# One core, attention beside a gated feed-forward: query loads issued one at a time, and new orders for the work of a unit

## The chip, the cores and the metric

The kernel runs on one NeuronCore of one Trainium2 chip. The metric is the device time of one execution in microseconds (us). Five engines run their own instruction streams in order and meet at semaphores: PE multiplies matrices (PEld is its weight load), DVE reduces, ACT applies exponentials and copies, POOL does elementwise work, and SP issues transfers between memory and the on-chip buffers.

## The reference

Both halves take the same x of 2048 tokens and 512 features, and everything is float32.

```
q = x @ wq   (32 heads of 16)      k = x @ wk, v = x @ wv  (one head of 16, shared)
p = softmax(q k^T / 4)             a = (p v) @ wo
b = ((x @ w_gate) * (x @ w_up)) @ w_down          (inner size 1792)
g = sigmoid(sum(x * gate_w))       out = g * a + (1 - g) * b
```

The scores are 32 x 2048 x 2048. Each needs its row's maximum first, then an exponential, then a product with v.

## The kernel before

**Units.** Attention is cut into 64 units. A unit `u` is eight heads (group `g`) of 128 query tokens (tile `t` of chunk `c`). Its queries stand in a buffer `Q[u]` with four slots of 128 columns in each of two halves of 64 partitions. There are `QB = 5` such buffers, so unit `u` reuses the buffer of unit `u - 5`.

**Three passes per unit.** `p1` multiplies queries with 512 keys (64 rows of the array, one half of the partitions) and DVE takes the row maximum (`mx`, L765 and L766). When 32 such tiles are done, `p1_end` folds them to one maximum per row, and SP writes it to memory in four pieces (`dm<-mt`, L786) and reads it back into two rows of each half of `Q[u]` (`Q<-dm`, L793). Thus `p2` computes score minus maximum in one product (L806), and ACT takes the exponential into `P` (L807). `pv` multiplies `P` with `V` into one bank `acc` (L819), four matrices side by side of 32 columns each, and ACT copies the result out as `osb` (L823).

**Fill.** Between these matmuls PE does the projections and the feed-forward as jobs (L965), each of which owns one of the eight PSUM banks until ACT has copied it (`gs`, L575, or `yt` and `y`, L399 and L396, which scale a result by its gate).

**The order.** PE's order is written out as strings of tokens. `a` and `b` are a `p1` matmul on the lower and the upper half of the partitions, `c` and `d` a `p2` matmul on these halves, `e` and `f` a fill matmul on them, and `p` is one step of `pv`, which the profile records as eight matmuls. Two matmuls on different halves run side by side; two on the same half follow each other. `ORDER` is one unit (144 tokens: 16 each of a, b, c and d, 36 each of e and f, 8 p). `ORDER_NINE` is a pair of units (288 tokens) and is used whenever a block of `down` jobs with nine products is ready (`nine_unit`), which happens for eight pairs. `ORDER_LAST` is the last pair. So 46 units follow `ORDER`, and 16 follow `ORDER_NINE`.

**The planner.** While the program is built, a planner keeps its own clock: each token advances it by fixed costs (`LANE` is the time between two matmuls of one half). Actions that aren't tokens, transfers among them, are put into a list by `later(ns, fn)` and are issued when that clock has passed. The clock is only an estimate: at run time SP issues its transfers in the order in which the planner recorded them, each when its semaphores allow.

**The query loads.** `place` calls `q_fetch(u)` when the buffer's old unit is through its `p2`. `q_fetch` issues two small transfers that clear the maximum rows (`Q<-dz`, L226) and six that bring the queries (`Q<-dq`, L233). It records in `qat` when the planner may count on them.

Of the kernel before, what the change touches and what calls it, by code (L numbers as in the profile page):

```python
# [14 lines left out]
F32 = mybir.dt.float32  # L15
# [7 lines left out]
DH = 16  # L23
# [9 lines left out]
PBUF = 13  # L33
WB = 4
QB = 5
LANE = 232.0
NEXT = 3.0
LOADW = 132.0
GAP = 50.0
# [9 lines left out]


ORDER = (
    "cdefedafcfebefedafeedafcfedebefadebefcfefefebededebefadfefcfadeefebedcfa"
    "fcfcfafefefafafcfefafcfedcfafafefedebcfebefebebebcbppppcdadcbppdababcppb"
)
ORDER_NINE = (
    "cbecffadeefdefafccfbeedbeefdafefcacfefebefebededaffebcefedafcffcfafefafe"
    "afdefedafecffeadcfefbedefadcpppdcdadcppcbcbadpppbcbcbefefcfefcfadedebede"
    "febcfebfefebedebedeebcfebedefafedefcfafcfafefedebafedefedfafecfaffcbefcf"
    "edadefafebefabapppadfcfebefcfedafefcbebefedefadefefebefcfabappbcbabapppb"
)  # L60
ORDER_LAST = (
    "cdebefebefefedededebbcfefefebefedaefefefadcfefafcfefafefedadefebefedefcf"
# [9 lines left out]
def mix_kernel(ctx: ExitStack, tc: tile.TileContext, x, wq, wk, wv, wo, wg, wu, wd, gw, out):  # L72
    nc = tc.nc
# [46 lines left out]
    clock = {"T": 0.0, "dve": 0.0, "act": 0.0, "pool": 0.0}  # L120
# [3 lines left out]
    def later(ns, fn):  # L124
        heapq.heappush(events, (clock["T"] + ns, next(serial), fn))
# [25 lines left out]
    def mm_all(p, prods, start=True, stop=True):  # L151
        for i, (l, r) in enumerate(prods):
            nc.tensor.matmul(p, l, r, start=start and i == 0, stop=stop and i == len(prods) - 1)  # L153
# [6 lines left out]
    def bank(i, name):  # L160
        return psum.tile([128, 512], F32, name=name, tag=f"bank{i}")

    def ms_bank(i):
        return bank(i, f"ms{i}")
# [51 lines left out]
    qat = {}  # L216

    Q = {u: work.tile([128, 4, 128], F32R, name="Q", tag="Q", bufs=QB) for u in range(QB)}
    dz = dram.tile([2, 512], F32, name="dz", bufs=1)

    def q_fetch(u):
        c, g, t = units[u]
        if u >= QB:
            Q[u] = Q[u - QB]
            for r in (48, 112):
                nc.sync.dma_start(Q[u][r:r + 2].rearrange("p s q -> p (s q)").bitcast(F32), dz)  # L226
        q = Q[u]
        for d, rows in zip(dq[c, g], ((0, 32), (16,))):
            for half in range(2):
                for r in rows:  # L230
                    b = half * 64 + r
                    src = d[half * 64:half * 64 + 64, t * 128:(t + 1) * 128]
                    nc.sync.dma_start(q[b:b + 16].bitcast(F32), src.rearrange("(s d) q -> d s q", d=DH))  # L233
        qat[u] = clock["T"] + 6000.0

    kvn = work.tile([128, 4, 32], F32, name="kvn", tag="oT", bufs=2)
    nc.scalar.dma_start(kvn[:, :, 0:16], wk_v)
# [209 lines left out]
    class State:  # L447
# [11 lines left out]
        def issue(self, l, wait):  # L459
# [3 lines left out]
            at = max(self.nl[l], self.last + NEXT, ldw + LOADW)  # L463
            self.nl[l] = at + LANE
            self.pd = max(ldw + 5.0, at - LANE)
            self.last = at
# [361 lines left out]
    p = bank(6, "warm")  # L828
# [3 lines left out]
    p = bank(6, "gwb")  # L832
# [8 lines left out]
    p = ms_bank(1)  # L841
# [3 lines left out]
    for u in range(2):  # L845
        q_fetch(u)
# [17 lines left out]
    p = ms_bank(0)  # L864
# [112 lines left out]
    def place(op):  # L977
        nonlocal fetched
        events_until(E.last if E.inpv else min(E.nl))
        if (fetched < NU and min(E.n2) >= NJ * (fetched - QB + 1) and fetched <= min(E.n1) // NJ + 2  # L980
                and (fetched != 3 or 0 in mat) and dqat.get(units[fetched][:2], 1e18) <= clock["T"]):
            later(1500, lambda n=fetched: q_fetch(n))
            fetched += 1
        if op == "p":
            at = E.npv
            E.pv()
            pv(at)
            return
        kind, l = divmod("abcdef".index(op), 2)
        if kind == 0:  # L990
            k = E.n1[l]
            if k < NS:
                wait_for(lambda: qat.get(order1[k][0], 1e18) <= clock["T"] + 200.0)
                b = E.s1(l)
                clock["dve"] = E.dve
                p1(k, l, b)
                E.dve = max(E.dve, clock["dve"])
                st["idle"] = min(E.n1) == NS
            elif fillable(l):
                fill(l)  # L1000
        elif kind == 1:
            k = E.n2[l]
            wait_for(lambda: mat.get(k // NJ, 1e18) <= clock["T"] + 200.0)
            p2(k, l, E.s2(l))
        elif not st["idle"] or fillable(l) or l == 1 and pos[1] < len(run):
            fill(l)
# [92 lines left out]
    while events or front or st["gen"] or st["next"]:  # L1099
        run_events()  # L1100
        if peek():
            j = take()
            items = j.prods()
            p = j.p
            if p is None:
                p = ms_bank(turn)
                turn = 1 - turn
            mm_all(p, items, j.start, j.evac is not None)
            clock["T"] += LANE * len(items)
            if j.evac:  # L1110
# [20 lines left out]
```

## Time and profile before

| | |
|---|---|
| median of 3 runs | 1583.41 us (1583.24 to 1583.56) |
| the profiled execution | 1583.97 us, its span 1582.2 us |
| PE, DVE, ACT, POOL busy | 1575.3, 1358.8, 1198.8, 734.5 us |
| L765, L806, L819, matmuls | 2048, 2048, 4096 |
| SP: `Q<-dq`, `Q<-dz`, `dm<-mt`, `Q<-dm` | 384, 118, 256 and 128 transfers |

A busy engine is not an engine at its best: the matmuls are pipelined, and a matmul that starts late shows as no idle time as long as the one before it is still running. Starts are therefore the better measure: the distance from one start to the next, and from the first `acc` of one unit to that of the next.

### The profile page before, as it was taken

What the parts mean: (1) busy time and instruction counts of PE and PEld (TensorE: products, weight loads), DVE (VectorE), ACT (ScalarE), POOL (GpSimd) and SP (SyncE); (2) the same over time, 40 slices, a digit from 0 to 9 for tenths busy, and PEclk for the clock granted to TensorE, in tenths of its full rate; (3) what the DMA queues carried; (4) which work ended last, traced back from release to release, by engine and by line L of the source; (5) the groups of instructions that cost most, each with busy time, mean ns of one, the idle gap of its engine ahead of it and who ended that gap; (6) DMA issues with size and microseconds to landing.
All of it is one profiled execution on the core that took longest, in us unless ns stands there. A gap on an engine that the chain in (4) does not pass through costs nothing.

```text
span 1582.2 us, 35723 instructions
## 1 busy us (share of the span) xinstructions
PE 1575.3 (100%) x13144; PEld 1026.6 (65%) x13144; DVE 1358.8 (86%) x2411; ACT 1198.8 (76%) x2384; POOL 734.5 (46%) x876
## 2 busy tenths in 40 slices
PE   9999999999999999999999999999999999999999
PEld 7775666665665666666665666676665666676665
DVE  6998989898888989898888889898888989898982
ACT  5786787877787787877787787877777786877776
POOL 8535636253633624454532625445443525545340
PEclk9999999999999999999999999999999999999999
DMA  6553322122232212121232212122132222212111
GB/s 197 188 177 119 94 63 74 43 69 60 68 104 80 75 49 74 43 87 55 61 104 72 75 56 74 50 69 66 55 117 65 69 61 75 61 57 59 36 32 42
DMA packets 185472, 121.71 MB, mean 77 GB/s; under 512 B 46435, under 2 KB 154851, under 8 KB 185298
## 3 DMA queue, kind: packets, MB, share of 16 engines
q1 hardware_dynamic: 184096, 119.10, 25.1%
q8 instruction: 104, 1.70, 0.4%
q14 instruction: 70, 0.57, 0.1%
q10 hardware_dynamic: 1202, 0.33, 0.1%
HBM read 83.18 MB, written 36.18 MB: 75 GB/s over the span
## 4 chain that ended last, share of the span: by engine, by line
PE 98%; DVE 1%; SPq 0%; issue 0%; DMA 0%; ACT 0%; POOL 0%; POOLq 0%
PE ms L965 33%; PE acc L819 29%; PE s L806 17%; PE s L765 17%; PE ms L153 1%; DVE mx L766 1%; PE ms L1055 1%; PE px L288 0%; SPq L233 0%; PE warm L830 0%; PE wo L153 0%; DMA Q<-dm 0%; PE pv L330 0%; SPq L786 0%; PE pick L730 0%
## 5 line engine op out<-in xcount | busy, mean ns | idle before, releaser
L766 DVE TENSOR_REDUCE mx<-s 128x1 f32<-128x512 f32 x2048 | 1285.1, 684 | 171.8 <-PE s L765 91.9
L807 ACT ACTIVATE P<-s 128x512 f32<-128x512 f32 x2048 | 1058.3, 648 | 258.8 <-PE s L806 217.3
L765 PE MATMUL s<-KK,Q 64*128 64x512 f32 x2048 | 702.5, 400 | 0.3
L806 PE MATMUL s<-Q,KK 64*128 64x512 f32 x2048 | 695.7, 404 | 1.5 <-DVE mx L766 0.8
L819 PE MATMUL acc<-P,V 128*32 128x512 f32 x4096 | 478.8, 597 | 0.0
L806 PEld LDWEIGHTS s<-Q,KK 64*128 64x128 f32 x2048 | 351.1, 184 | 133.0 <-ACT P L807 49.8
L765 PEld LDWEIGHTS s<-KK,Q 64*128 64x128 f32 x2048 | 350.5, 184 | 104.4 <-issue 52.0
L965 PE MATMUL ms<-xh,wl 64*128 64x512 f32 x896 | 314.6, 391 | 0.0
L965 PE MATMUL ms<-xh,wh 64*128 64x512 f32 x896 | 311.6, 392 | 0.0
L965 PE MATMUL ms<-xl,wh 64*128 64x512 f32 x896 | 300.4, 389 | 0.0
L819 PEld LDWEIGHTS acc<-P,V 128*32 128x32 f32 x4096 | 117.7, 109 | 254.2 <-issue 221.2
L586 POOL TENSOR_TENSOR hf<-gs 128x512 f32<-128x512 f32 x56 | 72.1, 1287 | 214.5 <-ACT gs L575 214.5
L965 PEld LDWEIGHTS ms<-xh,wh 64*128 64x128 f32 x896 | 159.2, 184 | 13.8 <-issue 0.5
L684 POOL TENSOR_TENSOR oT<-raw,rb 128x128 f32<-128x128 f32 x63 | 28.9, 459 | 288.2 <-DMA rb<-dr 279.2
L965 PE MATMUL ms<-wdh,hl 64*128 64x512 f32 x448 | 161.0, 391 | 0.0
L965 PEld LDWEIGHTS ms<-xh,wl 64*128 64x128 f32 x896 | 155.5, 184 | 7.6
L965 PE MATMUL ms<-wdh,hh 64*128 64x512 f32 x448 | 159.6, 390 | 0.0
L965 PEld LDWEIGHTS ms<-xl,wh 64*128 64x128 f32 x896 | 149.8, 184 | 8.8
L141 POOL TENSOR_TENSOR wl<-wn,wh 128x512 fp32r<-128x512 f32 x116 | 149.2, 1286 | 9.3
L400 POOL TENSOR_TENSOR y<-y,yt 128x512 f32<-128x512 f32 x58 | 74.7, 1288 | 169.3 <-ACT yt L399 160.7
L965 PE MATMUL ms<-wdl,hh 64*128 64x512 f32 x448 | 152.7, 390 | 0.0
L823 ACT COPY osb<-acc 128x512 f32<-128x512 f32 x64 | 37.6, 587 | 95.1 <-PE acc L819 95.1
(180 smaller groups left out, 1377.2 us busy)
## 6 DMA issues: line engine op xcount, KB each, us to landing
do<-osb SPq DMA_DIRECT2D x63, 256.0 KB
wn<-in_B_w_gate_dram SPq DMA_DIRECT2D x56, 256.0 KB
wn<-in_B_w_up_dram SPq DMA_DIRECT2D x56, 256.0 KB
wdn<-in_B_w_down_dram SPq DMA_DIRECT2D x56, 256.0 KB
Q<-dq SPq DMA_DIRECT2D x384, 32.0 KB
raw<-do SPq DMA_DIRECT2D x252, 32.0 KB
dq<-oh SPq DMA_DIRECT2D x16, 256.0 KB
dq<-ol SPq DMA_DIRECT2D x16, 256.0 KB
```

What stands on the lines that cost most here:

```text
L141: nc.gpsimd.tensor_tensor(lo, src, hi.bitcast(F32), op=OP.subtract)
L153: nc.tensor.matmul(p, l, r, start=start and i == 0, stop=stop and i == len(prods) - 1)
L400: nc.gpsimd.tensor_tensor(y[c, t], y[c, t], tmp, op=OP.add)
L586: nc.gpsimd.tensor_tensor(hf, gu[0], gu[1], op=OP.mult)
L684: nc.gpsimd.tensor_tensor(dst, raw[:, 0], rb, op=OP.mult)
L765: nc.tensor.matmul(p, q[r, slot], KK[r, kq * 512:(kq + 1) * 512], start=True, stop=True)
L766: nc.vector.tensor_reduce(mx[u][:, half * 4 + slot, kq:kq + 1], p, axis=AX.X, op=OP.max)
L806: nc.tensor.matmul(p, KK[r, j * 128:(j + 1) * 128], q[r].rearrange("p s q -> p (s q)"), start=True, stop=True)
L807: nc.scalar.activation(P[s][:, half], p, AF.Exp, scale=0.25)
L819: nc.tensor.matmul(acc[u][b:b + 32, :], V[:, j + i], src[:, half], start=(j == 0), stop=(j == NJ - 2))
L823: nc.scalar.copy(osb, acc.pop(u))
L965: nc.tensor.matmul(j.p, lhs[HALVES[l]], rhs[HALVES[l]], start=(l == 0 and i == 0), stop=(l == 1 and end))
```

## The change

`q_fetch` collects its two or no `dz` transfers and its six `dq` transfers in a list, issues the first, and puts each next one 1000 ns of the planner's clock behind the one before. (The first two units still issue all at once.) `qat` is 4000 ns behind the last one, not 6000 ns behind the burst. `LANE` goes from 232 to 229. `ORDER` and `ORDER_NINE` are replaced by other arrangements of the same tokens. No matmul, no reduction, no activation and no transfer is added or removed.

```
-LANE = 232.0
+LANE = 229.0
 ORDER = (
...
-    "fcfcfafefefafafcfefafcfedcfafafefedebcfebefebebebcbppppcdadcbppdababcppb"
+    "fcffafcfefafedefafebcfefcfafcfcfafebefcbefededebebcpppdcbcbappabcbcbpppb"
...
     def q_fetch(u):
         c, g, t = units[u]
+        parts = []
         if u >= QB:
             Q[u] = Q[u - QB]
             for r in (48, 112):
-                nc.sync.dma_start(Q[u][r:r + 2].rearrange("p s q -> p (s q)").bitcast(F32), dz)
+                parts.append((Q[u][r:r + 2].rearrange("p s q -> p (s q)"), dz))
...
-                    nc.sync.dma_start(q[b:b + 16].bitcast(F32), src.rearrange("(s d) q -> d s q", d=DH))
-        qat[u] = clock["T"] + 6000.0
+                    parts.append((q[b:b + 16], src.rearrange("(s d) q -> d s q", d=DH)))
+
+        def step(i):
+            nc.sync.dma_start(parts[i][0].bitcast(F32), parts[i][1])
+            if i + 1 < len(parts):
+                later(1000.0, lambda: step(i + 1))
+            else:
+                qat[u] = clock["T"] + 4000.0
+        if u >= 2:
+            step(0)
+        else:
+            for dst, src in parts:
+                nc.sync.dma_start(dst.bitcast(F32), src)
+            qat[u] = clock["T"] + 6000.0
```

The new file has 13 more lines ahead of the passes, so L786 reads L799 there, L819 reads L832, and so on.

**SP, the maxima of one early unit.** Here `dz` and `dq` are the query load of a later unit, and `dm` is the maximum on its way out (L786) and back (L793). Before:

```order
L226 DMA Q<-dz 2x512 x2
L233 DMA Q<-dq 16x4x128 x6
L786 DMA dm<-mt 8x2x32 x4
L179 DMA wn<-in_B_w_up_dram 128x4x128
L212 DMA dq<-oh 128x512
L212 DMA dq<-ol 128x512
L676 DMA dr<-rc 128x8
L793 DMA Q<-dm 2x512 x2
```

Now:

```order
L237 DMA Q<-dz 2x512
L179 DMA wn<-in_B_w_up_dram 128x4x128
L799 DMA dm<-mt 8x2x32 x4
L237 DMA Q<-dz 2x512
L237 DMA Q<-dq 16x4x128
L212 DMA dq<-oh 128x512
L212 DMA dq<-ol 128x512
L689 DMA dr<-rc 128x8
L237 DMA Q<-dq 16x4x128
L806 DMA Q<-dm 2x512 x2
```

Eight transfers of the query load stood ahead of the four writes of the maximum; now one does. Between the writes and the read back stand four other transfers before, and six now.

**PE, the end of a unit that follows ORDER.** `acc` rows count matmul instructions, four to a `p` token. Before:

```order
L819 MATMUL acc<-P,V 32x512 x16
L806 MATMUL s_2799<-Q,KK 128x512
L806 MATMUL s_2802<-Q,KK 128x512
L765 MATMUL s_2805<-KK,Q 128x512
L806 MATMUL s_2809<-Q,KK 128x512
L806 MATMUL s_2812<-Q,KK 128x512
L765 MATMUL s_2815<-KK,Q 128x512
L819 MATMUL acc<-P,V 32x512 x8
```

Now:

```order
L832 MATMUL acc<-P,V 32x512 x12
L819 MATMUL s_2791<-Q,KK 128x512
L819 MATMUL s_2795<-Q,KK 128x512
L778 MATMUL s_2798<-KK,Q 128x512
L819 MATMUL s_2801<-Q,KK 128x512
L778 MATMUL s_2804<-KK,Q 128x512
L778 MATMUL s_2807<-KK,Q 128x512
L832 MATMUL acc<-P,V 32x512 x8
```

Both go on with six matmuls and a third group, of 8 instructions before and of 12 now. A unit's eight steps of `pv` were grouped 4, 2, 2 and are grouped 3, 2, 3.

**PE, the end of the first unit of a pair that follows ORDER_NINE.** Before:

```order
L819 MATMUL acc<-P,V 32x512 x12
L806 MATMUL s_3551<-Q,KK 128x512
L806 MATMUL s_3554<-Q,KK 128x512
L806 MATMUL s_3558<-Q,KK 128x512
L765 MATMUL s_3561<-KK,Q 128x512
L806 MATMUL s_3565<-Q,KK 128x512
L806 MATMUL s_3568<-Q,KK 128x512
L819 MATMUL acc<-P,V 32x512 x8
L806 MATMUL s_3581<-Q,KK 128x512
```

Now:

```order
L832 MATMUL acc<-P,V 32x512 x12
L819 MATMUL s_3561<-Q,KK 128x512
L819 MATMUL s_3565<-Q,KK 128x512
L819 MATMUL s_3569<-Q,KK 128x512
L778 MATMUL s_3572<-KK,Q 128x512
L978 MATMUL ms_3432<-wdh,hh 128x512
L778 MATMUL s_3576<-KK,Q 128x512
L832 MATMUL acc<-P,V 32x512 x4
L819 MATMUL s_3585<-Q,KK 128x512
```

Before, the pair's groups of `pv` are 3, 2, 3 and 3, 2, 3 steps; now they are 3, 1, 2, 2 and 4, 2, 2, one group more. Two tokens of the same half stand side by side 27 times in the old pair and 47 times in the new one, 3 times and twice in the old and the new `ORDER`.

More of the change, by code (lines that the diff above doesn't have):

```diff
@@ L51 @@
 ORDER = (
-    "cdefedafcfebefedafeedafcfedebefadebefcfefefebededebefadfefcfadeefebedcfa"
-    "fcfcfafefefafafcfefafcfedcfafafefedebcfebefebebebcbppppcdadcbppdababcppb"
+    "cafedebedefedebedefadefcfafefadefedafcfafefebedefefadefcbefedebedafefeda"
+    "fcffafcfefafedefafebcfefcfafcfcfafebefcbefededebebcpppdcbcbappabcbcbpppb"
 )
 ORDER_NINE = (
[L56 to L59, printed above, removed]
+    "cfeadcfafefedefedafcfafedefedebefedafefbefedacfefcbeffcafefedafeffebdedf"
+    "eaebcfedefaefedafcfafefebedefcfebcfebcbpppdcdafapdcfabcppbcbcbeppcbfacff"
+    "eefbeedbefeddeaefedafedbefcfeedafcfebeffefebdfeebdecaeffcafdefafcbeedefe"
+    "dfacffafebfeceffadeafcffecfaffcfacfebefebedebebebcbppppdadcbappadcbabppb"
 )
```

## The prediction

> **What bounds the kernel now.** I read the page first, then the chain of waits, then single stretches.
>
> ```profile
> PE 1575.3 (100%) x13144; PEld 1026.6 (65%) x13144; DVE 1358.8 (86%) x2411; ACT 1198.8 (76%) x2384; POOL 734.5 (46%) x876
> PEclk9999999999999999999999999999999999999999
> PE 98%; DVE 1%; SPq 0%; issue 0%; DMA 0%; ACT 0%; POOL 0%; POOLq 0%
> ```
>
> PE carries the chain from end to end, at the full clock. The change adds no PE work, so it can only alter the distances between PE's starts. The chain in order of time shows each unit's first group of `acc`; two neighbours give a unit's length. Cut at such marks, the instructions on the tile `yt` (columns: stretch, its length, busy us and count on ACT, then on POOL, clock, DMA share, GB/s) show eight units that follow `ORDER`:
>
> ```profile
> 785.25 3.57 PE acc L819 x32
> 808.85 3.63 PE acc L819 x32
> ```
>
> ```profile
> 714.12:737.82 23.70, 1.48 (x2) 1.29 (x1) 1.00 0.21 60
> 737.82:761.63 23.81, 1.59 (x2) 3.87 (x3) 1.00 0.16 46
> 761.63:785.25 23.62, 0.00 (x0) 0.00 (x0) 1.00 0.26 71
> 785.25:808.85 23.60, 0.74 (x1) 0.00 (x0) 1.00 0.30 90
> 808.85:832.67 23.82, 2.37 (x3) 3.86 (x3) 1.00 0.37 113
> 832.67:856.51 23.84, 1.58 (x2) 3.87 (x3) 1.00 0.23 71
> 856.51:880.13 23.62, 0.00 (x0) 0.00 (x0) 1.00 0.24 69
> 880.13:903.76 23.63, 0.00 (x0) 0.00 (x0) 1.00 0.29 81
> ```
>
> Units without a `yt` take 23.62 us; of the four with two or three, one takes 23.70 and three 23.8, with the same work on PE. A `yt` is a longer copy on ACT, so ACT reaches PE although its mean share is 76%. The next rows (stretch, length, then busy us and count of PE, PEld, DVE, ACT, POOL) say where:
>
> ```profile
> 761.60:765.10 3.50, 3.50 (x34) 0.90 (x32) 3.42 (x8) 0.60 (x1) 2.17 (x3) 1.00 0.05 12
> 774.00:778.00 4.00, 4.00 (x38) 3.79 (x37) 4.00 (x7) 4.00 (x9) 1.18 (x1) 1.00 0.18 36
> 778.00:782.00 4.00, 4.00 (x39) 3.70 (x36) 3.99 (x7) 4.00 (x10) 3.78 (x5) 1.00 0.26 71
> ```
>
> In the first group of `pv`, four steps long, ACT has one instruction in 3.5 us: it starves. From 774 to 782 us ACT and DVE are both busy without a break. They catch up there, and a PSUM bank that either frees late delays the matmul that needs it. The mean share hides a starved stretch and a saturated one.
>
> **The price of a group, and the floor of a unit.** PE's starts in one of these units:
>
> ```profile
> 761.56 3.64 PE L819 MATMUL acc<-P,V 128*32 128x512 f32 x32
> ...
> 766.03 1.92 PE L819 MATMUL acc<-P,V 128*32 128x512 f32 x16
> ...
> 768.78 1.92 PE L819 MATMUL acc<-P,V 128*32 128x512 f32 x16
> 770.63 0.50 PE L765 MATMUL s<-KK,Q 64*128 64x512 f32 x1
> ...
> 770.97 0.62 PE L965 MATMUL ms<-xh,wh 64*128 64x512 f32 x2
> ...
> 773.05 0.39 PE L965 MATMUL ms<-xh,wh 64*128 64x512 f32 x1
> ...
> 774.19 0.39 PE L965 MATMUL ms<-xh,wh 64*128 64x512 f32 x1
> ...
> 784.86 0.39 PE L765 MATMUL s<-KK,Q 64*128 64x512 f32 x1
> 785.18 3.64 PE L819 MATMUL acc<-P,V 128*32 128x512 f32 x32
> ```
>
> Four `p` and six matmuls take 766.03 - 761.56 = 4.47 us, two `p` and six matmuls 768.78 - 766.03 = 2.75. So a `p` is (4.47 - 2.75) / 2 = 0.86, and a group with its six matmuls costs 2.75 - 1.72 = 1.03 beyond its steps. From 773.05 to 774.19 a half of the array makes five steps of 0.228. Six matmuls, three on each half, would cost 0.68 in a long run, so one more group costs 1.03 - 0.68 = 0.35.
>
> The long run of 124 matmuls, 62 on each half, lasts 785.18 - 770.63 = 14.55. Its 61 steps at 0.228 are 13.91, the first is 770.97 - 770.63 = 0.34 and so 0.11 longer, and the turn into `acc` is 785.18 - 784.86 = 0.32. That makes 14.34: this unit loses 0.21 of its 23.62 us. The eight units' mean is 189.64 / 8 = 23.705 (their sum over their number), 0.085 more, so the mean loss is 0.295.
>
> **The change, part by part.**
>
> *Units that follow `ORDER` (46).* Same matmuls, same three groups, same floor. The longest starvation falls from four `p` to three, which hands ACT 0.86 us of its backlog earlier. The 0.085 that `yt` brings is a tenth of that, so I let it vanish. The other 0.21 belongs to DVE's backlog as well, whose 32 reductions per unit are untouched; of it I take a sixth, 0.035. 0.12 x 46 = **-5.5 us**. Bounds: nothing, and the whole loss, 0.295 x 46 = 13.6. The value lies nearer to the small end because only the `yt` rows show a loss that moves with ACT's load.
>
> *Pairs that follow `ORDER_NINE` (8).* One more group each, +0.35; the long runs are better balanced between the halves, one step less (137 against 136, counted as the larger half of each run), -0.23. Twenty more same-half neighbours can each cost what the halves are apart at that moment. The rows below show two halves 0.07 apart:
>
> ```profile
> 776.03 0.39 PE L965 MATMUL ms<-xh,wh 64*128 64x512 f32 x1
> 776.10 0.39 PE L806 MATMUL s<-Q,KK 64*128 64x512 f32 x1
> ```
>
> ```profile
> 903.76:975.10 71.34, 71.34 (x604) 46.22 (x608) 62.12 (x112) 55.08 (x109) 28.50 (x36) 1.00 0.21 62
> ```
>
> After such a neighbour the halves are in step again, so the price is not paid 20 times: bounds 0 and 20 x 0.07 = 1.4, and I take 0.15. The last row is a pair with the unit behind it, 71.34. Sum 0.35 - 0.23 + 0.15 = 0.27, x 8 = **+2.2 us**.
>
> *Query loads one by one.* Two stalls of PE stand out.
>
> ```profile
> 119.38 3.92 SPq L233 DMA_DIRECT2D Q<-dq  x6
> 123.75 1.60 SPq L786 DMA_DIRECT2D dm<-mt  x4
> ...
> 127.56 0.61 SPq L793 DMA_DIRECT2D Q<-dm  x2
> ```
>
> ```profile
> 128.89 0.50 PE L765 MATMUL s<-KK,Q 64*128 64x512 f32 x1
> 130.10 0.62 PE L806 MATMUL s<-Q,KK 64*128 64x512 f32 x2 [0.71 <-DMA Q<-dm]
> ```
>
> ```profile
> 1172.08 0.57 SPq L793 DMA_DIRECT2D Q<-dm  x2
> ```
>
> ```profile
> 1173.80 0.50 PE L765 MATMUL s<-KK,Q 64*128 64x512 f32 x1
> 1175.13 0.60 PE L806 MATMUL s<-Q,KK 64*128 64x512 f32 x2 [0.83 <-DVE mx L766]
> ```
>
> ```profile
> 1171.62 2.48 DVE L766 TENSOR_REDUCE mx<-s 128x1 f32<-128x512 f32 x4 [1.26 <-PE s L765]
> ```
>
> The writes of the maximum left SP right behind the six-fold load, which held SP for 3.92 us; the read back landed 130.10 - 127.56 = 2.5 after its issue, and `p2` waited. The second row names DVE, but those four reductions were over at 1171.62 + 2.48 = 1174.10, a microsecond before the matmul; the read back, issued at 1172.08 to 1172.65, fits the same 2.5. The stalls are 1.21 and 1.33 less a step: 0.98 + 1.10. With one transfer of the load ahead of the writes instead of eight, SP is some 3 us earlier (3.92 x 5 / 6), more than either stall. **-2.1 us**; bounds 0 and 2.1, since no other start is that late. On the other side, six transfers among the writes and the read back, each some 0.4 to 0.65 us of SP, stand where four stood: at most 1.3 us of the 3 gained.
>
> *`LANE` and the new `qat`.* They issue nothing; they shift where timed transfers fall among the tokens. Start and end of the program keep their matmuls. I cost them at nothing, covered by the five query buffers; were that cover gone, a late query load would hold `p1` by one fetch, some 4 us once.
>
> Sum: -5.5 + 2.2 - 2.1 = -5.4. The profiled execution took 1583.97 us, so it would take 1578.6. The median of the runs is 0.56 lower, which makes **1578.0 us**.
>
> **The rivals.** A change of 0.2%, 3.2 us, is about what a measurement here can tell from none.
>
> *DVE sets the saturated stretch.* DVE is at 86% and has 4.00 and 3.99 of 4.00 us in the rows above, so relief for ACT moves nothing. Against it: lengths that follow `yt`, which DVE doesn't touch. Then -0.03 x 46 + 2.2 - 2.1 = -1.3: 1582.1. The Trainium skill's page Perfetto Trace Analysis, section Identifying the Most-Contended Engine, points the same way: it judges TensorE by its weight loads' share (65% here) and not by matmul busy time, and takes the engine with the highest occupancy, which would be DVE. I don't follow it all the way, because PE's starts keep within 0.3 us of their floor in each unit.
>
> *The pairs cost full price (slower).* If halves drift apart again before each new neighbour, a pair pays 0.35 - 0.23 + 1.4 = 1.5, and 8 pairs 12.2: -5.5 + 12.2 - 2.1 = +4.6, 1588.0. It decides from 7.6 / 8 = 0.95 per pair on. For it: a group of four `p` appears in each pair where three was the longest. Against it: the old pair already has 27 neighbours, and its two units and the next one take 71.34, only 0.22 more than three units of 23.705.
>
> *All of the loss goes.* With shorter starvation neither ACT nor DVE ever saturates: -0.25 x 46 + 2.2 - 2.1 = -11.4, 1572.0. Against it: DVE's load.
>
> *The loads still come in bursts.* The planner's 1000 ns are not the chip's, and SP may bunch them again; the stalls stay: 1580.1.
>
> **How the numbers follow.** Forecast 0.42, bursts 0.10, DVE 0.25, full price 0.11, all of the loss 0.12. Around the forecast a gain per unit of 0.06 to 0.18 gives 1575.2 to 1580.8. The range, 1572.8 to 1585.0, leaves out most of the largest gain and of the slower case. Faster by over 0.2% (below 1580.2): 0.40 of the forecast, half of the bursts, the largest gain, 0.05 of DVE's, together 0.62. Within 0.2%: 0.26. Slower: 0.12.
>
> **What would show it.** `ORDER` units near 23.58 instead of 23.705, and no longer by two lengths with and without `yt`; ACT with breaks in the run after the last group. Pairs near 71.5 with the next unit. No start of `p2` 1 us late, `dm<-mt` within a microsecond or two of its reductions. I am wrong if units without a `yt` stay at 23.62 (then DVE or PE itself holds them), if pairs exceed 72.2, or if a `p2` waits on its maximum elsewhere.

## The result and the profile after

| | before | after |
|---|---|---|
| median of 4 runs | 1583.49 us (1583.24 to 1583.89) | 1575.24 us (1574.07 to 1575.34) |
| the profiled execution, its span | 1583.97, 1582.2 us | 1575.34, 1573.6 us |

The ratio is 0.9946, 95% interval 0.9933 to 0.9958: 8.3 us faster. The forecast was 1578.0 within 1572.8 to 1585.0, so the sign and the range held; the gain is half as large again as the 5.4 forecast, and its main term came about in another way than the prediction said.

From the page of the changed kernel, the busy times and the chain of waits by engine:

```profile
PE 1568.0 (100%) x13144; PEld 1022.0 (65%) x13144; DVE 1328.4 (84%) x2411; ACT 1208.7 (77%) x2384; POOL 734.3 (47%) x876
PE 96%; ACT 1%; DVE 0%; issue 0%
```

Same counts of instructions, same engine on the chain. As in the prediction, a unit is measured from its first `acc` to the next unit's. Eight `ORDER` units of the changed kernel, cut at these marks, with the instructions on the tile `yt` (stretch, its length, ACT busy and count, POOL busy and count, clock, DMA share, GB/s):

```profile
711.62:735.03 23.41, 1.39 (x2) 1.30 (x1) 1.00 0.23 65
735.03:758.46 23.43, 1.44 (x2) 3.86 (x3) 1.00 0.15 42
758.46:781.92 23.46, 0.00 (x0) 0.00 (x0) 1.00 0.26 76
781.92:805.36 23.44, 0.68 (x1) 0.00 (x0) 1.00 0.33 98
805.36:828.80 23.44, 2.12 (x3) 3.86 (x3) 1.00 0.37 110
828.80:852.23 23.43, 1.44 (x2) 3.86 (x3) 1.00 0.21 65
852.23:875.66 23.43, 0.00 (x0) 0.00 (x0) 1.00 0.26 75
875.66:899.13 23.47, 0.00 (x0) 0.00 (x0) 1.00 0.27 77
```

Before, the same stretch had 23.62 without a `yt` and 23.70 to 23.84 with two or three. Now each of these eight takes 23.44 within 0.03, whatever its `yt`. The change removes more than the `yt` surplus: the units without a `yt` lose 0.18 too, and those were to stay nearly as they were.

**Where the 8.6 us of span went.** Each unit can be measured in both traces in this way. 37 units follow `ORDER` and stand outside the pairs, the units behind them and the last three. Without the few that hold a stall their mean goes from 23.694 to 23.449. A pair with the unit behind it goes from 71.347 to 71.563 (means of eight). The parts below are differences of such means; the pair's price, 0.38, is taken from the runs below, and the stretch of the unit behind a pair changes by what is left of 71.563 - 71.347 = 0.216.

| part | predicted | in the two traces |
|---|---|---|
| `ORDER` units | -5.5 | 37 x -0.245 = -9.1, and 8 x (0.216 - 0.38) = -1.3 behind pairs: -10.4 |
| `ORDER_NINE` pairs | +2.2 | 8 x 0.38 = +3.0 |
| two late read backs | -2.1 | units 2 and 46 were 1.06 and 1.37 too long and are not now: -2.4 |
| start and end | 0 | first `acc` 0.35 later, unit 1 0.72 too long, last three units 0.05: +1.1 |
| sum | -5.4 | -8.7 (the spans differ by 8.6) |

### The profile page after: what moved, and what is told of

Same layout as the page of the kernel before. It is cut to its first block, busy times and chain, and to the rows that moved or that the text cites. A ratio compares the mean times of both kernels' runs of the same rounds, so it can differ in the third digit from the quotient of the medians.

```text
span 1573.6 us, 35557 instructions
## 1 busy us (share of the span) xinstructions
PE 1568.0 (100%) x13144; PEld 1022.0 (65%) x13144; DVE 1328.4 (84%) x2411; ACT 1208.7 (77%) x2384; POOL 734.3 (47%) x876
## 4 chain that ended last, share of the span: by engine, by line
PE 96%; ACT 1%; DVE 0%; issue 0%
PE ms L978 32%; PE acc L832 30%; PE s L778 18%; PE s L819 16%; ACT P L820 0%; PE wo L153 0%; PE ms L1068 0%; ACT gs L588 0%; PE pick L743 0%; ACT osb L836 0%; DVE mx L779 0%; DVE y L754 0%; ACT gs L388 0%; ACT yt L361 0%; DVE gg L378 0%
## 5 line engine op out<-in xcount | busy, mean ns | idle before, releaser
L779 DVE TENSOR_REDUCE mx<-s 128x1 f32<-128x512 f32 x2048 | 1255.8, 682 | 193.1 <-PE s L819 125.8
L820 ACT ACTIVATE P<-s 128x512 f32<-128x512 f32 x2048 | 1069.8, 630 | 225.7 <-PE s L819 114.4
L819 PE MATMUL s<-Q,KK 64*128 64x512 f32 x2048 | 742.7, 402 | 0.0
L778 PE MATMUL s<-KK,Q 64*128 64x512 f32 x2048 | 714.1, 400 | 0.5
L832 PE MATMUL acc<-P,V 128*32 128x512 f32 x4096 | 480.5, 597 | 0.0
L819 PEld LDWEIGHTS s<-Q,KK 64*128 64x128 f32 x2048 | 356.6, 184 | 97.7 <-ACT P L820 50.9
L978 PE MATMUL ms<-xl,wh 64*128 64x512 f32 x896 | 312.9, 387 | 0.0
L978 PE MATMUL ms<-xh,wh 64*128 64x512 f32 x896 | 304.3, 389 | 0.0
L832 PEld LDWEIGHTS acc<-P,V 128*32 128x32 f32 x4096 | 113.3, 109 | 257.9 <-issue 215.7
L978 PEld LDWEIGHTS ms<-xl,wh 64*128 64x128 f32 x896 | 156.5, 184 | 7.7
L978 PEld LDWEIGHTS ms<-xh,wh 64*128 64x128 f32 x896 | 152.5, 184 | 10.5 <-issue 0.2
L978 PE MATMUL ms<-wdh,hh 64*128 64x512 f32 x448 | 152.7, 389 | 0.0
L978 PE MATMUL ms<-wdh,hl 64*128 64x512 f32 x448 | 151.8, 388 | 0.0
```

The source lines that it names most:

```text
L778: nc.tensor.matmul(p, q[r, slot], KK[r, kq * 512:(kq + 1) * 512], start=True, stop=True)
L779: nc.vector.tensor_reduce(mx[u][:, half * 4 + slot, kq:kq + 1], p, axis=AX.X, op=OP.max)
L819: nc.tensor.matmul(p, KK[r, j * 128:(j + 1) * 128], q[r].rearrange("p s q -> p (s q)"), start=True, stop=True)
L820: nc.scalar.activation(P[s][:, half], p, AF.Exp, scale=0.25)
L832: nc.tensor.matmul(acc[u][b:b + 32, :], V[:, j + i], src[:, half], start=(j == 0), stop=(j == NJ - 2))
L978: nc.tensor.matmul(j.p, lhs[HALVES[l]], rhs[HALVES[l]], start=(l == 0 and i == 0), stop=(l == 1 and end))
```

## The experiments

All times are medians; "against before" is the ratio to runs of the old kernel on the same chip, with its 95% interval.

### The change taken apart

**The new `ORDER` alone**, in the old kernel:

```
-    "cdefedafcfebefedafeedafcfedebefadebefcfefefebededebefadfefcfadeefebedcfa"
-    "fcfcfafefefafafcfefafcfedcfafafefedebcfebefebebebcbppppcdadcbppdababcppb"
+    "cafedebedefedebedefadefcfafefadefedafcfafefebedefefadefcbefedebedafefeda"
+    "fcffafcfefafedefafebcfefcfafcfcfafebefcbefededebebcpppdcbcbappabcbcbpppb"
```

> The kernel before with the new ORDER alone (old pairs, loads in a burst, LANE 232). In the two traces a unit under ORDER goes from 23.70 to 23.44 us outside single stalls. If the new order alone does that, 46 units give 46 x 0.26 = 12.0 us: 1571.5, or 1573.6 if the two late read backs of the maximum stay elsewhere. Rival: the units are shorter because the loads no longer come in a burst or because the planner's clock differs; then this run stays above 1579.

Measured: 1572.92 us, 0.9932 (0.9915 to 0.9948), so -10.4 us from this string alone. `ORDER` units take 23.460, with no difference by `yt` (23.469 without, 23.451 with two or three). The smaller of the two late read backs is still there (0.61 us between two starts of PE at 130.0); the other is not. The first `acc` comes 0.45 late, much as in the full change (0.35), so the loss at the start comes with this string.

**The new `ORDER_NINE` alone**, in the old kernel (only that string is replaced):

> The kernel before with the new ORDER_NINE alone. The traces give 71.35 us before and 71.56 after for a pair with the unit behind it, of which that unit has won 0.26, so a pair costs 0.48 more: 8 x 0.48 = 3.8, 1587.3. By the prediction's term it would be 2.2, 1585.7. Rival: the pairs are no worse by themselves and only suffer from what stands around them; then 1583.5.

Measured: 1585.38 us, 1.0012 (1.0003 to 1.0022). A pair with its next unit takes 71.718 instead of 71.347: +0.37, or +3.0 for eight. The median rose by only 2.0, mainly because this kernel's stalls at the late read backs shrank on their own (0.65 us between two starts at 129.9, none above 0.6 near 1175).

**The loads one by one alone**, in the old kernel (`q_fetch` of the change, `LANE` and orders as before):

> The kernel before with query loads one by one alone. Theory: the two stalls of PE on a late maximum go, 2.1 us: 1581.4, and units stay at 23.6 to 23.8. Rival: the stalls go but others come, or the planner's clock moves them: 1583.5. If the loads in a burst had also slowed the units, 1575 or less.

Measured: 1582.37 us, 0.9994 (0.9985 to 1.0003), profiled 1582.44 against 1583.97. Both stalls are gone from the trace; no two starts of PE between the first unit and the end of the last are more than 0.6 us apart. The interval includes no change, so the time alone doesn't prove the gain of 1 to 1.5 us; the trace shows its place. That is less than the two stalls together (2.4 us in the trace of before): units elsewhere, pairs among them, came out slightly longer.

**The change with the old pairs**: the changed kernel with the old `ORDER_NINE`.

> The changed kernel with the old ORDER_NINE. If the pairs cost 0.48 each, this is 3.8 us faster than the change: 1571.4, and its ORDER units stay at 23.44. If the new pairs are needed beside the new ORDER, 1575 or more.

Measured: 1572.51 us (1572.45 to 1572.62), 0.9931 (0.9916 to 0.9945), a pair with its next unit 71.185 against 71.563 with the new pairs. So the new pair costs 0.38 here as well, and **this version has the lowest median of all**: 10.8 us below the kernel before and 2.7 below the change. The two ratios' intervals overlap (the change, measured apart, had 0.9933 to 0.9958), so the lead over the change rests on the pairs' lengths in the traces. Against the new `ORDER` alone it gains only 0.4 us by the loads one by one and the new `LANE`; `LANE` by itself was not tried.

### What in ORDER gives the gain

The prediction said: the groups of `pv` go from 4, 2, 2 to 3, 2, 3 steps, so ACT starves for a shorter time. The rival: the arrangement of the other tokens does it. These two kernels cross the two.

**New arrangement, old groups**, in the changed kernel:

```
-    "...ebcpppdcbcbappabcbcbpppb"
+    "...ebcppppdcbcbappabcbcbppb"
```

> The changed kernel with the pv steps of ORDER grouped 4, 2, 2 again (one p moved from the third group to the first), all else the new order. Starvation theory (the prediction's): a group of four starves ACT, so units under ORDER lengthen to 23.6 or more and depend on yt again: 1575.2 + 46 x 0.2 = 1584. Rival: the arrangement of the long run is what counts, and units stay at 23.45: 1575.2.

**Old arrangement, new groups**, in the old kernel:

```
-    "...bcbppppcdadcbppdababcppb"
+    "...bcbpppcdadcbppdababcpppb"
```

> The kernel before with the pv steps of ORDER grouped 3, 2, 3 (one p moved from the first group to the third), all else the old order. Starvation theory: units go to 23.45 whatever their yt: 1583.3 - 46 x 0.22 = 1573. Rival, the long run counts: units stay at 23.6 to 23.8, 1583.3.

Measured: 1581.97 us for the first, 0.9992 (0.9982 to 1.0001), and 1593.04 for the second, 1.0066 (1.0051 to 1.0081). Neither theory had the second slower. One unit without `yt` of each of the four kernels says why. It is cut in two: from the first `acc` to the first matmul after the third group, and from there to the next unit's first `acc` (stretch, length, then busy us and count of PE, PEld, DVE, ACT, POOL, clock, DMA share, GB/s). The kernel before:

```profile
761.56:770.63 9.07, 9.07 (x78) 2.83 (x76) 6.93 (x14) 3.76 (x7) 2.67 (x4) 1.00 0.26 69
770.63:785.18 14.55, 14.55 (x128) 12.60 (x124) 14.12 (x25) 14.30 (x29) 7.98 (x9) 1.00 0.25 71
```

The changed kernel:

```profile
758.46:767.54 9.08, 9.08 (x80) 2.75 (x78) 6.61 (x13) 4.24 (x8) 2.53 (x4) 1.00 0.26 68
767.54:781.92 14.38, 14.38 (x129) 12.71 (x125) 13.75 (x25) 14.06 (x28) 7.81 (x9) 1.00 0.26 81
```

New arrangement with groups 4, 2, 2:

```profile
761.62:770.82 9.20, 9.20 (x79) 2.85 (x78) 6.44 (x13) 4.24 (x8) 2.52 (x4) 1.00 0.27 75
770.82:785.21 14.39, 14.39 (x126) 13.36 (x124) 13.88 (x26) 14.13 (x28) 7.82 (x9) 1.00 0.25 75
```

Old arrangement with groups 3, 2, 3:

```profile
765.87:775.18 9.31, 9.31 (x79) 2.92 (x77) 7.21 (x14) 3.76 (x7) 2.63 (x4) 1.00 0.22 67
775.18:789.71 14.53, 14.53 (x128) 12.51 (x124) 13.84 (x24) 14.31 (x29) 7.96 (x9) 1.00 0.24 71
```

Read the ACT column first. With the old arrangement ACT does 7 instructions between the groups and 29 in the long run, with the new one 8 and 28, *whatever the groups are*. The traces show these counts in every `ORDER` unit from the eleventh on outside the pairs and before the last three, 32 in each of the four kernels. And the long run follows the arrangement, not the groups: 14.55 and 14.53 with 29, 14.38 and 14.39 with 28. The prediction's floor for it was 14.34, so the new arrangement leaves 0.04 of loss. The groups cost something only where they don't fit: 9.07 and 9.08 us for each kernel's own, 9.20 and 9.31 for the crossed ones.

The timeline of ACT shows where the eighth instruction comes from (start, us, operation, count, idle time before it and what ended it). ACT in the kernel before, around its first group at 761.56:

```profile
761.65 0.60 ACT L807 ACTIVATE P<-s 128x512 f32<-128x512 f32 x1 [0.17 <-PE s L765]
765.67 2.06 ACT L807 ACTIVATE P<-s 128x512 f32<-128x512 f32 x4 [3.42 <-PE s L806]
```

ACT in the changed kernel, around its first group at 758.46:

```profile
759.62 1.57 ACT L820 ACTIVATE P<-s 128x512 f32<-128x512 f32 x3 [1.30 <-PE acc L832]
761.70 1.58 ACT L820 ACTIVATE P<-s 128x512 f32<-128x512 f32 x3 [0.51 <-PE s L819]
```

Before, ACT does one exponential and then waits 3.42 us for scores that PE can only make after the group. Now ACT waits for `pv` to release a `P` buffer: three scores stand ready in PSUM when the group begins, and ACT takes them during the group. (Counted as matmuls at L806 or L819 started, less exponentials started, at the first `acc`: one in each of the 32 units of the old arrangement, three in each of the new.) So one exponential, worth 0.49 us in a row of several ((1.57 - 0.60) / 2), moves out of the stretch where ACT is busy for 14.30 of 14.55 us.

The timeline explains the crossed groups too. ACT with the old arrangement and groups 3, 2, 3:

```profile
765.98 0.60 ACT L807 ACTIVATE P<-s 128x512 f32<-128x512 f32 x1 [0.21 <-PE s L806]
769.12 2.06 ACT L807 ACTIVATE P<-s 128x512 f32<-128x512 f32 x4 [2.54 <-PE s L806]
```

and PE of the same kernel at that place:

```profile
769.30 0.49 PE L765 MATMUL s<-KK,Q 64*128 64x512 f32 x1
769.72 1.92 PE L819 MATMUL acc<-P,V 128*32 128x512 f32 x16
```

The shorter first group did cut ACT's wait, from 3.42 to 2.54 us, by 0.88, about the 0.86 that the prediction named. But the exponential of 769.12 ends 0.60 later, at 769.72, and there the second group starts, 0.42 behind the matmul before it instead of 0.32. It looks as if `pv` waits for that exponential, since the first group ended a step earlier. From the first matmul behind the first group to the second group these units take 1.12 us instead of 0.90, which is nearly all that they lose. The 0.86 handed to ACT is not a gain when `pv` needs the result at once. In the other crossed kernel (new arrangement, 4, 2, 2) the loss lies in the third group: its two steps take 1.99 us instead of 1.85, and ACT's last two exponentials, from 768.70 to 769.78, end inside it.

**Same-half neighbours.** Ten `ef` or `fe` of the new `ORDER` are swapped so that 22 tokens have a neighbour of the same half instead of 2 (the first line of the string; same counts of tokens):

```
-    "cafedebedefedebedefadefcfafefadefedafcfafefebedefefadefcbefedebedafefeda"
+    "cafedebedfeedebedfeadfecfaeffadfeedafcfaeffebedfeefadfecbfeedebedaeffeda"
```

> The changed kernel with ten pairs of e and f swapped in the long run of ORDER, 22 same-half neighbours instead of 2, all else as changed. If a neighbour costs what the halves are apart but sets them in step again, as predicted for the pairs (0.15 us for twenty), units lengthen by 0.15: 1575.2 + 46 x 0.15 = 1582. If the halves are in step anyway, nothing: 1575.2. If each costs 0.07, 1575.2 + 46 x 1.4 = 1640.

Measured: 1582.02 us, 0.9992 (0.9982 to 1.0001); `ORDER` units 23.594, +0.145. That is the size that the prediction gave twenty neighbours in a pair (0.15). It isn't paid twenty times, though, but at one place. Take, in each long run, the start of its k-th matmul (counted from 0) less that of the first, less 0.2275 for each two matmuls, and average over the units without a `yt`: with the swap this loss is 0.16 at matmul 37 and 0.36 at matmul 43, and stays there. In the changed kernel it is 0.16 and 0.16. Units with two or three `yt` lose less at this place (0.16 and 0.27).

**One token moved in the old ORDER**, which takes two of its three neighbours away (in the old kernel):

```
-    "...ebefadfefcfadeefebed..."
+    "...ebefadefefcfadefebed..."
```

> The kernel before with one token of the old ORDER moved: the e behind the second pair of neighbours in the middle of the long run goes eight places ahead, so that the two same-half neighbours there are gone and one at the start is left. In the trace of before, PE's starts at these two places lose some 0.05 us each per unit. Theory (neighbours after the halves have drifted apart): 0.1 less per unit, 1583.3 - 46 x 0.1 = 1578.7. Rival (ACT sets the run): the loss only moves to the next wait, 1583.3, and units with three yt stay 0.2 longer than those with none.

Measured: 1583.79 us, 1.0006 (0.9997 to 1.0015). Units without `yt` 23.654, with two or three 23.817, as before (23.644 and 23.803). Those two neighbours are not the old order's loss.

**Where the old order loses.** The same loss along the long run, in us. "With `yt`" means one or more; unit 46 of the kernel before, whose long run holds the late read back, is left out:

| kernel, units | matmul 7 | 25 | 67 | 97 | 103 | 121 |
|---|---|---|---|---|---|---|
| before, no `yt` | 0.12 | 0.16 | 0.25 | 0.30 | 0.32 | 0.34 |
| before, with `yt` | 0.12 | 0.16 | 0.27 | 0.32 | 0.42 | 0.46 |
| after, no `yt` | 0.12 | 0.16 | 0.19 | 0.18 | 0.18 | 0.17 |
| after, with `yt` | 0.12 | 0.17 | 0.20 | 0.19 | 0.18 | 0.18 |

Old: the opening, a creep over the rest of the run, and with a `yt` a jump of 0.10 behind matmul 97 (0.14 in the units with two or three). New: little more than the opening. One such jump in the kernel before, in the timeline of PE:

```profile
829.38 0.39 PE L965 MATMUL ms<-wdh,hh 64*128 64x512 f32 x1
829.63 0.50 PE L765 MATMUL s<-KK,Q 64*128 64x512 f32 x1
829.97 0.39 PE L765 MATMUL s<-KK,Q 64*128 64x512 f32 x1
```

and ACT of the same kernel there:

```profile
828.24 0.85 ACT L399 ACTIVATE yt<-ms,gb 128x512 f32<-128x512 f32 x1
828.81 2.73 ACT L807 ACTIVATE P<-s 128x512 f32<-128x512 f32 x5
```

Two halves that were staggered start together at 829.63 and take 0.34 to the next start instead of 0.228. The exponential behind the `yt` began at 828.81; the row of five, at 0.49 apart, leaves 2.73 - 4 x 0.49 = 0.77 for one, so it ended at 829.58, 0.05 ahead of that matmul. The bank that it frees fits the wait; that it is this bank is read from the times alone.

### Which engine reaches PE

**One more copy on ACT per unit**, of the unit's result onto itself, in the old kernel and in the changed one:

```
 nc.scalar.copy(osb, acc.pop(u))
+nc.scalar.copy(osb, osb)
```

> The kernel before with one more ACT instruction per unit, a copy of osb onto itself at the start of the long run, some 0.5 us; PE's order is the same. If ACT's backlog reaches PE under the old order, as the units with yt suggest (0.07 us for each 0.09 us more on ACT), units lengthen by up to 0.4: 1583.3 + 64 x 0.4 = 1609. If ACT has room, 1583.3.

> The changed kernel with the same added ACT copy per unit. If the new order leaves ACT room, as its units of 23.44 whatever their yt suggest, it stays near 1575.2, at most 0.1 per unit more, 1581. If ACT is as tight as under the old order, 1601.

Measured: 1622.3 us, 1.0247 (1.0231 to 1.0262), and 1613.22, 1.0188 (1.0173 to 1.0203). Per unit of `ORDER` without `yt` that is 24.281 - 23.644 = 0.64 and 24.060 - 23.445 = 0.62: all of a copy of 0.62 us, in both. I had expected the changed kernel to hide most of it. The changed kernel with the copy, timeline of ACT at the start of a long run:

```profile
760.86 0.59 ACT L836 COPY osb<-acc 128x512 f32<-128x512 f32 x1 [1.90 <-PE acc L832]
761.47 0.62 ACT L837 COPY osb<-osb 128x512 f32<-128x512 f32 x1
762.00 4.50 ACT L820 ACTIVATE P<-s 128x512 f32<-128x512 f32 x9
```

and PE of the same kernel there:

```profile
762.21 0.39 PE L979 MATMUL ms<-wdh,hl 64*128 64x512 f32 x1
762.64 0.50 PE L819 MATMUL s<-Q,KK 64*128 64x512 f32 x1
762.98 0.39 PE L778 MATMUL s<-KK,Q 64*128 64x512 f32 x1
```

A `p2` matmul starts at 762.64, when the first exponential behind the copies is over (762.00 + 0.60): 0.43 after the start before it, 0.20 more than a step. The loss along the run is 0.12 at matmul 7 and 0.71 at matmul 19, against 0.12 and 0.14 without the copy, and grows by only 0.09 after that. With the copy in the kernel before it is 0.12 and 0.70 at these places, too. So right behind the groups PE has no room left for ACT in either kernel.

**One more reduction on DVE per unit**, of 128x512, in the old kernel at the same place:

```
 nc.scalar.copy(osb, acc.pop(u))
+nc.vector.tensor_reduce(work.tile([128, 1], F32, name="dx", bufs=2), KK[:, 0:512].bitcast(F32), axis=AX.X, op=OP.max)
```

> The kernel before with one more DVE reduction per unit at the same place, 128x512 from the on-chip buffer, some 0.6 us; PE's order is the same. If DVE sets the saturated stretch (the prediction's rival), units lengthen by up to 0.6: 1583.3 + 64 x 0.6 = 1622. If ACT alone does, 1583.3 to 1590.

Measured: 1584.2 us, 1.0009 (1.0 to 1.0019); units without `yt` 23.658 against 23.644. A reduction of 0.67 us costs about 0.01. DVE, at 86% and busy for 14.12 of the long run's 14.55 us, has room; ACT, at 76%, has none at this place. The Trainium skill's page Perfetto Trace Analysis, section Identifying the Most-Contended Engine, would take the engine of highest occupancy beside TensorE, which is DVE; the two measured prices disagree with it here.

### The pairs

**The pair's single step merged into the next group**, in the changed kernel (the first unit's groups become 3, 3, 2, not the 3, 2, 3 that the expectation names):

```
-    "...bcbpppdcdafapdcfabcppbcbcbepp..."
+    "...bcbpppdcdafadcfabcpppbcbcbepp..."
```

> The changed kernel with the single p of ORDER_NINE moved into a group of two (3, 2 and 3 come out of 3, 1, 2 and 2 in the pair's first unit), so a pair has six groups as before. If the extra group is the pair's surplus at its price, 0.35 us each with nothing else, 8 x 0.35 = 2.8 less: 1572.4. If what follows only waits for ACT instead, 1575.2 or more.

Measured: 1581.46 us, 0.9991 (0.9982 to 1.0), so 6.2 above the change instead of 2.8 below it. A pair with its next unit takes 72.327, +0.76. Each of its eight pairs has one place like this, in the timeline of PE:

```profile
216.12 0.39 PE L778 MATMUL s<-KK,Q 64*128 64x512 f32 x1
216.79 0.81 PE L819 MATMUL s<-Q,KK 64*128 64x512 f32 x2 [0.28 <-ACT P L820]
```

and ACT of the same kernel there:

```profile
216.14 3.04 ACT L820 ACTIVATE P<-s 128x512 f32<-128x512 f32 x6 [2.38 <-PE s L819]
```

ACT had waited 2.38 us for a score; its exponential ends at 216.14 + 0.60 = 216.74, and PE, which needs the bank, goes on at 216.79, 0.67 after the start before. The extra group seemed a waste of 0.35; without it PE and ACT wait for each other there, and the pair is longer.

**What the new pair pays.** In the traces the old pair and the new one can be laid side by side run by run (means of the eight pairs; the kernel before against the one with only the new pairs). The turns from a long run into a first group of `pv` take 0.41, 0.39 and 0.32 in the old pair and its next unit, 0.47, 0.45 and 0.34 with the new: +0.14. The rest, 0.37 - 0.14 = +0.23, is the extra group and the long runs together. One such turn in the changed kernel, in the timeline of PE:

```profile
592.68 0.46 PE L778 MATMUL s<-KK,Q 64*128 64x512 f32 x1
593.15 0.64 PE L832 MATMUL acc<-P,V 128*32 128x512 f32 x4
```

and ACT of the same kernel there:

```profile
591.81 0.79 ACT L588 COPY gs<-ms 128x512 f32<-128x512 f32 x1
592.27 0.82 ACT L820 ACTIVATE P<-s 128x512 f32<-128x512 f32 x1
```

The group starts at 593.15, 0.06 after an exponential that stood behind a copy ends (592.27 + 0.82 = 593.09), and 0.47 after the matmul before it instead of 0.32.

## Why the prediction was right or wrong, step by step

**What bounds the kernel: right in the engine.** ACT's lateness reaches PE's distances, while DVE has room. The prediction argued this from lengths that follow `yt`; the copy at full price and the reduction at about none show it. The rival in which DVE sets the stretch falls. The place is less sure: the copy is paid for right behind the groups, and in the saturated stretch itself the old order's jumps behind a `yt` are the only loss that the traces tie to ACT.

**`ORDER` units, -5.5: right in sign, wrong in its lever and size.** The step that failed is "The longest starvation falls from four `p` to three, which hands ACT 0.86 us of its backlog earlier". The 0.86 is there in the trace with only the groups changed, and brings nothing: with the old arrangement the shorter groups cost 9.8 us (1593.04 against 1583.28 on its chip). What works is the arrangement of the other tokens: with it three scores stand ready for ACT when the first group begins, and one exponential moves out of the long run, with 3, 2, 3 and with 4, 2, 2 alike. That the arrangement and not the grouping shortens the long run is shown by the crossed kernels; that it does so by these three scores is argued from the counts. For the same reason the sixth of the other 0.21 was too little: that loss wasn't DVE's, and nearly all of it left (0.04 remains above the floor). Per unit -0.245 came instead of -0.12, the size of the rival "all of the loss goes" (-0.25). The prediction weighed that rival down with "DVE's load", which is the reading that the reduction refutes. It showed the starved stretch (0.60 of 3.50 us) and counted the steps in the group, but never counted how many scores stand ready when the group begins; the rows of ACT around the group, or the order of the tokens ahead of the first `p`, would have told it.

**That the time fell into the range is partly luck.** The `ORDER` units gave 4.9 us more than forecast, which by itself would have made 1573.1, at the edge of the range. The pairs, 0.8 dearer, and a loss of 1.1 at the start that had no term brought it back towards the forecast.

**The sign "ACT with breaks in the run after the last group": wrong for most of the run.** The same four-microsecond stretches of the changed kernel (columns as above):

```profile
770.00:774.00 4.00, 4.00 (x38) 3.62 (x36) 4.00 (x7) 4.00 (x9) 0.28 (x1) 1.00 0.09 19
774.00:778.00 4.00, 4.00 (x39) 3.85 (x38) 4.00 (x8) 4.00 (x9) 3.78 (x5) 1.00 0.28 85
778.00:782.00 4.00, 4.00 (x40) 3.23 (x40) 3.90 (x9) 3.74 (x8) 3.84 (x5) 1.00 0.23 67
```

From 770 to 778 ACT and DVE have no break at all, and only in the last four microseconds 0.26 and 0.10 us are free. Yet hardly any matmul is late there (the table above). A stretch without a break is not yet a stretch that delays PE.

**Pairs, +2.2: right in sign, mis-sized.** Measured +0.37 and +0.38 per pair, +3.0. Group, balance and neighbours together were put at 0.27 and measured 0.23 (their sum alone, not each of them); what was missed is 0.14 in the turns, where the first group of the new pair waits for its last exponential.

**Loads one by one, -2.1: right in the mechanism, and in the traces of the whole change in the size too.** SP in the changed kernel, at the place of the first stall (start, us, transfer, count):

```profile
120.72 1.48 SPq L799 DMA_DIRECT2D dm<-mt  x4
122.24 0.26 SPq L237 DMA_DIRECT2D Q<-dz  x1
122.87 0.31 SPq L237 DMA_DIRECT2D Q<-dq  x1
...
124.66 0.46 SPq L237 DMA_DIRECT2D Q<-dq  x1
125.22 0.55 SPq L806 DMA_DIRECT2D Q<-dm  x2
```

The writes go out at 120.72 instead of 123.75, the 3 us earlier that the prediction worked out. The read back follows 125.22 - (120.72 + 1.48) = 3.0 behind them instead of 2.2, so the transfers in between took back 0.8 (at most 1.3 was allowed). No `p2` waits for it any more. The rival of the bursts falls with it. Alone, the loads gained 1.0 us by the median. At the start of the program the whole change loses: "I cost them at nothing" was wrong by about 1.1 us, of which the first `acc` (0.35) and unit 1 (0.72) have most. The new `ORDER` alone has most of both (first `acc` 0.45 later, unit 1 at 23.99). Unit 1 is not that string's alone, since it takes 24.07 and 24.11 in two kernels with the old arrangement (groups 3, 2, 3, and the added reduction). The chain of waits of the changed kernel leaves PE in unit 1 for an exponential on ACT and the gates on DVE (start, us, what):

```profile
105.60 0.60 ACT P L820
106.33 0.18 DVE gb L377
106.54 0.27 DVE gg L378
```

**The slower rival** (pairs at 1.5 each) fell: 0.38. In `ORDER` twenty neighbours cost one jump, not one each; in the pairs they were not tried by themselves.

**Open.** Which of the moved tokens has the three scores ready, and whether these scores alone make the gain, was not tried by itself: the two arrangements differ over the whole unit. The swapped neighbours show that other tokens count as well, for that kernel has three scores ready and 8 and 28 instructions, too, and still a longer run. That the creep of the old long run comes from ACT is argued from its 14.30 busy us of 14.55 and from the two arrangements; no run takes the creep away by relieving ACT alone. The jump in the units with the swapped tokens, at one place instead of at twenty, has no cause here.

## What to carry to other kernels

Ask of an engine that starves beside a long block not only how long the block is but how many inputs stand ready when it begins; that count, read in the rows of the starved engine (what ended its wait: a producer, or a free buffer), went with the gain here. Busy shares didn't tell which engine has room; one added instruction per unit on each did. An order and its grouping are fitted to each other, so cross them before crediting either, and take a bundled change apart: here one part gave 10 us and another took 3 back.

## What the runs showed of the hardware beyond what I expected

An ACT copy of 0.62 us added per unit lengthens a unit by 0.62 to 0.64 us in a kernel whose ACT is busy 76 to 77% of the time, while a DVE reduction of 0.67 us costs about 0.01 where DVE is busy 86%. Twenty more same-half neighbours among 124 matmuls cost 0.145 us on average, in one jump. Two exponentials of 128x512 on ACT start 0.49 us apart, though one alone takes 0.60.
